# First output tile finished and stored in column halves, and 8 KB store runs for two batches only

## The chip, the cores and the metric

The kernel runs on one core of a Trainium2 chip. The metric is the device time of one execution in microseconds (us); the lower, the better. Times quoted as "span" are of one profiled execution, from its first to its last instruction, and are 1.7 to 1.9 us shorter than the device time.

## The reference, cut to what matters

```python
# linear attention with elu+1 features -> x, shape (8, 576, 512); then:
X = np.fft.rfft(x, axis=1)                 # along the sequence
Y = np.zeros_like(X)
Y[:, :64] = X[:, :64] times w_r + i*w_i    # one complex 512x512 matrix per mode
u = x + np.fft.irfft(Y, n=576, axis=1)
out = u + np.maximum(u @ w_ch, 0.0)        # float32
```

## The kernel before

For 380 us the kernel streams the mode matrices (64 modes, two 1 MB matrices each) from HBM, the chip's main memory. Everything that doesn't need the last modes is done meanwhile: each output tile (128 rows x 512 columns) already holds x plus the inverse transform of most modes, and `E0` holds most of its channel product. The last 8 modes arrive at the end. Their rows are in `last`: `last[:, 0]` is the spectrum, `last[:, 1]` the same times `w_ch`. Then, for each pair of tiles, TensorE forms an accumulator in two banks of PSUM, the memory that TensorE writes its sums to (`channels`: E0 through an identity, then the inverse transform of the second part of `last` or of `YZ_all`, the copy of `last` spread out by batch). ScalarE rectifies it in place, TensorE adds the inverse transform of the first part, VectorE adds x, and SyncE stores the pair.

```python
    QUADS = (2, 4, 5, 6)        # batches whose 4 main tiles go in one store of 8 KB runs

    def finish(n: int):
        add_inverse(n, 0)
        ...
        on_bank(n, {0, 1}, nc.vector.tensor_tensor(out=x, in0=acc, in1=x, op=ALU.add))
        if t0 < B * NJJ and t0 // NJJ in QUADS:
            if t0 % NJJ:
                store(t0 - 2, NJJ)       # 1 MB, only when the second pair is done
            return
        store(t0, 2)                     # 0.5 MB, 4 KB runs

    # ---- the last modes have come; rows[] are their transposed spectrum
    for h in range(2):
        for ec in range(NDC):
            pin(nc.tensor.matmul(last_ps[h][:, 0:hw], rows[ec], wch16[:, ec, COLS[h]], ...))   # zl, then z1l
        pin(nc.scalar.copy(out=last[:, 1, COLS[h]], in_=last_ps[h][:, 0:hw]))
    pin(nc.tensor.matmul(y0, lead_sb[0][:, rows_of(0)], last[:, 0, :]))
    pin(nc.vector.tensor_tensor(out=x_of(0), in0=y0, in1=x_of(0), op=ALU.add))
    for h, eng in enumerate((nc.sync, nc.gpsimd)):
        eng.dma_start(out=YZ_all[...], in_=last...)
    psW.release()                        # y0's pool; its banks become accumulators 2 and 3
    ...
    add_inverse(0, 1)
    on_bank(0, {0}, nc.vector.scalar_tensor_tensor(      # x += max(acc, 0)
        out=x_of(0), in0=accs[0][:, 0], scalar=0.0, in1=x_of(0), op0=ALU.max, op1=ALU.add))
    store(0, 1)
    relu(0, 1)
    rectified(1)
    channels(2)
    ...
```

Also of interest later: `FILL` gives the number of filler matmuls after each pair of modes, which keep TensorE busy while it waits for weights.

```python
    FILL = {**{p: 5 for p in range(18, 27)}, 27: 8, 28: 2, 29: 7, 30: 7}
```

## Time and profile before

| | |
|---|---|
| device time, median of 4 runs | 425.81 us (424.87 to 425.96) |
| span of the profiled run | 422.9 us |
| last cast that the change doesn't reach (VectorE, 128x64 into Y) starts | 390.18 us |
| first store issued | 393.51 us |
| TensorE's last matmul ends | 414.3 us |
| last data packet ends | 421.5 us |

The cast into Y is the last step common to all kernels, so I measure from it: the **tail** is the stretch from its start to the end of the span, 32.74 us here.

These two rows of the page of before show 40 equal slices of the span, in tenths: the clock granted to TensorE, and the busy share of the 16 DMA engines.

```profile
...
PEclk9999778869855555555555598999799896899997
DMA  9999999999999999999999999999999999996797
...
```

DMA is busy nearly always: the kernel is bound by its transfers, and only the few slices at the end can be changed by this edit. The windows view of before cuts them finer. Each row gives a stretch in us, its length, each engine's busy time with its number of instructions, the granted clock, the DMA share and GB/s. (A packet counts whole in the stretch in which it starts, so a share can come out just over 1.)

```profile
...
core 0: us, PE busy (x) PEld busy (x) DVE busy (x) ACT busy (x) POOL busy (x), PEclk, DMA share, GB/s
398.00:400.00 2.00, 2.00 (x13) 0.53 (x10) 2.00 (x3) 1.72 (x5) 0.00 (x0) 1.00 0.96 384
400.00:401.00 1.00, 1.00 (x10) 0.34 (x9) 1.00 (x1) 0.76 (x2) 0.00 (x0) 1.00 0.90 365
401.00:402.00 1.00, 1.00 (x9) 0.28 (x8) 0.97 (x2) 0.86 (x3) 0.00 (x0) 1.00 0.26 107
402.00:403.00 1.00, 1.00 (x9) 0.27 (x6) 0.95 (x2) 0.98 (x2) 0.00 (x0) 1.00 0.99 418
403.00:420.00 17.00, 10.82 (x60) 2.67 (x56) 12.47 (x11) 9.64 (x18) 0.00 (x0) 0.90 1.00 400
420.00:421.00 1.00, 0.00 (x0) 0.00 (x0) 0.00 (x0) 0.00 (x0) 0.00 (x0) 0.50 0.07 29
421.00:422.00 1.00, 0.00 (x0) 0.00 (x0) 0.00 (x0) 0.00 (x0) 0.00 (x0) 0.50 0.03 12
...
```

There is a dry stretch: DMA share 0.26 in 401 to 402 us, because the 1 MB store of batch 2 waits for its second pair. From 402 to 420 us the transfers never stop. From 420 us a single engine is left (0.07 of 16 is about one).

The timeline of before at the start of the tail (start, length, engine, line, operation, tiles, shapes, count, and in brackets the idle time before with what ended it):

```profile
...
start us, us, engine line op out<-in xcount [idle before <-releaser]
...
391.77 0.37 ACT L918 CAST last<-z1l 128x256 f16<-128x256 f32 x1
391.99 0.69 DVE L920 TENSOR_TENSOR x_main<-y0l,x_main 128x512 f32<-128x512 f32 x1 [0.80 <-PE y0l L919]
392.17 0.64 SPq L922 DMA_DIRECT2D YZ_all<-last  x1
...
392.79 0.69 DVE L943 SCALAR_TENSOR_TENSOR x_main<-acc,x_main 128x512 f32<-128x512 f32 x1
...
393.05 0.59 PE L775 MATMUL acc<-E,id 128*128 128x512 f16 x2
...
393.51 0.34 SPq L791 DMA_DIRECT2D out_dram<-x_main  x1
393.92 0.69 DVE L937 TENSOR_TENSOR x_main<-acc,x_main 128x512 f32<-128x512 f32 x1 [0.44 <-PE acc L736]
```

ScalarE casts z1l at 391.77 us, which completes `last`; accumulator 2 starts on TensorE at 393.05 us (L775); VectorE makes two full passes over the first tile; SyncE copies `last` into YZ_all and then stores the first tile.

### The profile page before, as it was taken

How to read it: one execution, taken by the hardware profiler on the slowest of the kernel's cores; microseconds unless marked ns; L12 is line 12 of the kernel's file. 1: busy time of each engine (PE TensorE's matmuls, PEld its weight loads, DVE VectorE, ACT ScalarE, POOL GpSimd, SP SyncE). 2: the span in 40 equal slices, each digit the busy share in tenths (PEclk: the TensorE clock that was granted, in tenths of full speed). 3: DMA queues.
4: the chain of work that ended last, by engine and by line, in shares of the span. 5: the costliest groups of instructions: out<-in, count | busy, mean ns of one | idle time of the engine just before them, and what ended most of it. 6: DMA issues, size and time to landing. Idle time of an engine off the chain costs nothing.

```text
span 422.9 us, 7976 instructions
## 1 busy us (share of the span) xinstructions
PE 279.6 (66%) x3426; PEld 153.2 (36%) x3426; DVE 215.4 (51%) x446; ACT 161.7 (38%) x253; POOL 56.5 (13%) x99
## 2 busy tenths in 40 slices
PE   1358387788717645344344768878798886989991
PEld 0246366666402322222122333334243333465320
DVE  4599488886202453354444434454264333423892
ACT  4688578754201102000000234444254351331881
POOL 4222124210000111111011111110110001130000
PEclk9999778869855555555555598999799896899997
DMA  9999999999999999999999999999999999996797
GB/s 217 210 208 215 207 220 202 224 209 222 221 215 219 207 215 217 222 211 217 218 212 217 217 220 214 215 216 215 214 219 220 215 212 219 223 201 126 248 409 287
DMA packets 20227, 93.20 MB, mean 220 GB/s; under 512 B 2016, under 2 KB 11104, under 8 KB 15520
## 3 DMA queue, kind: packets, MB, share of 16 engines
q0 software_dynamic: 16512, 81.47, 94.0%
q1 hardware_dynamic: 3680, 11.22, 7.0%
q8 instruction: 27, 0.44, 0.4%
q14 instruction: 8, 0.07, 0.0%
HBM read 163.93 MB, written 9.44 MB: 410 GB/s over the span
## 4 chain that ended last, share of the span: by engine, by line
DMA 63%; PE 22%; DVE 4%; ACT 3%; issue 2%; POOL 2%; DVEq 0%; POOLq 0%; ACTq 0%
DMA w<-in_moe_w_i_dram 48%; DMA pick_sb<-row_pick 8%; PE P L442 7%; DMA k<-in_k_dram 7%; PE acc L736 3%; PE acc L775 2%; PE zl L425 2%; ACT ke L213 2%; POOL w L119 1%; PE eps L677 1%; DVE ys L452 1%; PE ya L654 1%; PE yt L460 1%; PE xTp L667 1%; PE z L699 1%
## 5 line engine op out<-in xcount | busy, mean ns | idle before, releaser
L442 PE MATMUL P<-w,xt_c 64*32 64x512 bf16 (+2 forms) x1000 | 50.2, 531 | 59.7 <-DMA w<-in_moe_w_i_dram 58.3
L452 DVE CAST ys<-P 128x512 f16<-128x512 f32 x32 | 22.1, 692 | 122.2 <-PE P L442 122.2
L454 ACT CAST ys<-P 128x512 f16<-128x512 f32 x31 | 18.1, 585 | 154.1 <-PE P L442 154.1
L119 POOL DMA_DIRECT2D w<-in_moe_w_r_dram x31 | 16.6, 534 | 246.2 <-PE P L442 96.4
L442 PEld LDWEIGHTS <-xt_c 64*32 64x32 bf16 (+2 forms) x1000 | 16.7, 127 | 79.8 <-DMA w<-in_moe_w_i_dram 44.6
L165 PEld LDWEIGHTS <-qT 64*128 64x128 f16 (+1 forms) x640 | 23.0, 123 | 49.8 <-issue 31.0
L677 PE MATMUL eps<-wch,xTw 128*128 128x512 f16 x144 | 40.2, 406 | 0.0
L165 PE MATMUL num<-kv,qT 64*128 64x65 f16 (+1 forms) x320 | 13.7, 209 | 25.4 <-ACT xt_c L350 12.0
L658 DVE TENSOR_TENSOR x_main<-ya,x_main 128x512 f32<-128x512 f32 x32 | 22.0, 689 | 13.4 <-PE ya L654 13.2
L660 ACT CAST x16w<-x_main 128x512 f16<-128x512 f32 x32 | 19.8, 618 | 23.4 <-DVE x_main L658 22.3
L165 PE MATMUL nw<-kv,qT 64*128 64x65 f16 (+1 forms) x320 | 19.0, 240 | 9.5 <-DVE x_tail L621 4.3
L685 ACT CAST E<-eps 128x512 f16<-128x512 f32 (+1 forms) x40 | 21.2, 540 | 8.5 <-PE eps L677 8.4
L299 DVE TENSOR_TENSOR x<-num,rd 128x512 f16<-128x512 f32 x32 | 22.1, 692 | 1.1
L242 PE MATMUL qTp<-id,qe 128*128 128x128 f16 x144 | 16.1, 301 | 9.9 <-DVE qe L226 9.4
L460 PE MATMUL yt<-pick_sb,ys 128*128 128x16 f16 x252 | 11.7, 174 | 16.3 <-DMA pick_sb<-row_pick 9.6
L213 ACT ACTIVATE qe<-q 128x1152 f16<-128x1152 f16 (+1 forms) x16 | 17.9, 1157 | 10.4 <-DMA q<-in_q_dram 6.5
L249 ACT COPY qT<-qTp 128x1152 f16<-128x1152 f16 x16 | 19.6, 1287 | 0.7 <-PE qTp L242 0.2
L425 PE MATMUL zl<-wch,id 128*128 128x512 f16 x72 | 19.6, 408 | 0.0
L213 ACT ACTIVATE ke<-k 128x1152 f16<-128x1152 f16 x16 | 17.7, 1152 | 4.9 <-DMA k<-in_k_dram 4.9
L460 PEld LDWEIGHTS <-ys 128*128 128x128 f16 x252 | 9.7, 102 | 26.4 <-DVE ys L452 15.0
L785 ACT ACTIVATE acc<-acc 128x512 f32<-128x512 f32 x34 | 18.1, 582 | 2.4 <-PE acc L736 1.6
L242 PEld LDWEIGHTS <-qe 128*128 128x128 f16 x144 | 13.8, 140 | 11.0 <-DVE qe L226 9.8
(113 smaller groups left out, 468.6 us busy)
## 6 DMA issues: line engine op xcount, KB each, us to landing
w<-in_moe_w_r_dram POOLq DMA_DIRECT2D x31, 1024.0 KB, 12.5
w<-in_moe_w_i_dram POOLq DMA_DIRECT2D x31, 1024.0 KB, 17.0
k<-in_k_dram POOLq DMA_DIRECT2D x8, 576.0 KB, 12.8
v<-in_v_dram POOLq DMA_DIRECT2D x8, 576.0 KB, 14.8
out_dram<-x_main SPq DMA_DIRECT2D x4, 1024.0 KB, 4.9
q<-in_q_dram POOLq DMA_DIRECT2D x7, 576.0 KB, 12.9
out_dram<-x_main SPq DMA_DIRECT2D x6, 512.0 KB, 4.6
q<-in_q_dram SPq DMA_DIRECT2D x2, 576.0 KB, 4.3
```

The lines of the kernel that those rows point to most:

```text
L119: nc.gpsimd.dma_start(out=w_in[p][half::2], in_=two.rearrange("g (r dc) e -> (g r) dc e", dc=NDW))
L165: mm = nc.tensor.matmul(num[hpo][orow, c0 : c0 + 65], qT[rows, hpp, h2, cols], kv_sb[rows, hpp, h2, :])
L213: pin(nc.scalar.activation(out=ev[:, c], in_=heads(nm, b, c), func=AF.Exp))
L242: nc.tensor.transpose(qT_ps[:, j], phi["q", b][:, c, j].rearrange("p o d -> p (o d)"), id16,)
L299: nc.vector.tensor_tensor(out=dst.rearrange("p (o c d) -> p o c d", o=2, c=4), in0=nv[:, :, :, 0:64], in1=rden.unsqueeze(3).broadcast_to([ ...
L425: pin(nc.tensor.matmul(last_ps[0], id16, wch16[:, 0, :]))
L442: nc.tensor.matmul(P[c : c + n, :], xt_cols(dc, kk, n), w[rows, dc, :], start=(dc < NDC), stop=(dc >= n_dc - NDC), tile_position=(rows.sta ...
L452: pin(nc.vector.tensor_copy(out=st, in_=P))
L460: nc.tensor.matmul(yt_ps[:, ec, kk % 8, :], st[:, ec * 128 : ec * 128 + 128], pick_sb)
L658: pin(nc.vector.tensor_tensor(out=x, in0=acc, in1=x, op=ALU.add))
L677: nc.tensor.matmul(e_ps, xT[:, c, :], wch16[:, c, :], start=(c == 0), stop=(c == NDC - 1))
L685: pin(nc.scalar.copy(out=dst, in_=e_ps[:, cols]))
```

## The change

The intent is to get the first store out sooner and to smooth the stores. The first tile is finished in two column halves. VectorE can then work on the first half while TensorE still completes the second, and to allow that the second half's sum gets a PSUM bank of its own. The Trainium skill ("PSUM — Partial Sum Buffer", Terms) says that TensorE writing and VectorE reading one bank and quadrant at once is a collision error. Batches 2 and 4 are stored pair by pair (4 KB runs), only 5 and 6 in 8 KB runs.

```diff
--- before.py
+++ after.py
@@ -799,7 +799,7 @@
             in_=x_tail[i // 2],
         )
 
-    QUADS = (2, 4, 5, 6)
+    QUADS = (5, 6)
 
     def finish(n: int):
         acc = accs[n]
@@ -907,6 +907,17 @@
         pin(nc.tensor.transpose(y_ps[ec // 2][:, ec % 2, :], rows[ec], id16))
     pin(nc.scalar.copy(out=last[:, 0, COLS[0]], in_=y_ps[0].rearrange("p c r -> p (c r)")))
     pin(nc.vector.tensor_copy(out=last[:, 0, COLS[1]], in_=y_ps[1].rearrange("p c r -> p (c r)")))
+    z0 = psW.tile([128, D], F32, tag="P", bufs=2, name="z0h1")[:, COLS[1]]
+
+    def second_half_sums():
+        pin(nc.tensor.matmul(z0, id16, e0_parts(0)[0][1][:, COLS[1]], start=True, stop=False))
+        pin(
+            nc.tensor.matmul(
+                z0, inv2_sb[0 : 2 * NF, rows_of(0)], YZ[0][0 : 2 * NF, 1, COLS[1]],
+                start=False, stop=False,
+            )
+        )
+
     for h in range(2):
         for ec in range(NDC):
             pin(
@@ -916,8 +927,29 @@
                 )
             )
         pin(nc.scalar.copy(out=last[:, 1, COLS[h]], in_=last_ps[h][:, 0:hw]))
-    pin(nc.tensor.matmul(y0, lead_sb[0][:, rows_of(0)], last[:, 0, :]))
-    pin(nc.vector.tensor_tensor(out=x_of(0), in0=y0, in1=x_of(0), op=ALU.add))
+        if h == 0:
+            pin(nc.tensor.matmul(y0, lead_sb[0][:, rows_of(0)], last[:, 0, :]))
+            second_half_sums()
+    for h in range(2):
+        x = x_of(0)[:, COLS[h]]
+        l, r = lead_sb[0][:, rows_of(0)], last[:, 1, COLS[h]]
+        if h == 0:
+            z = accs[0][:, 0, COLS[0]]
+            on_bank(0, {0}, nc.tensor.matmul(z, l, r, start=False, stop=True, skip_group_check=True))
+        else:
+            z = z0
+            pin(nc.tensor.matmul(z, l, r, start=False, stop=True))
+        pin(nc.vector.tensor_tensor(out=x, in0=y0[:, COLS[h]], in1=x, op=ALU.add))
+        ins = nc.vector.scalar_tensor_tensor(
+            out=x, in0=z, scalar=0.0, in1=x, op0=ALU.max, op1=ALU.add
+        )
+        if h == 0:
+            on_bank(0, {0}, ins)
+        else:
+            pin(ins)
+        nc.sync.dma_start(
+            out=out_rows[0:512, COLS[h]].rearrange("(r j) d -> r j d", j=NJJ)[:, 0, :], in_=x
+        )
     for h, eng in enumerate((nc.sync, nc.gpsimd)):
         eng.dma_start(
             out=YZ_all[64 * h : 64 * h + 64 : NF // NL].rearrange("r b z d -> r b (z d)"),
@@ -937,14 +969,7 @@
         on_bank(n, {i}, nc.vector.tensor_tensor(out=x_of(t), in0=accs[n][:, i], in1=x_of(t), op=ALU.add))
         store(t, 1)
 
-    add_inverse(0, 1)
-    on_bank(
-        0, {0},
-        nc.vector.scalar_tensor_tensor(
-            out=x_of(0), in0=accs[0][:, 0], scalar=0.0, in1=x_of(0), op0=ALU.max, op1=ALU.add
-        ),
-    )
-    store(0, 1)
+    add_inverse(0, 1, (1,))
     relu(0, 1)
     rectified(1)
     channels(2)
```

## The prediction

> **What bounds the kernel now.** On the page the DMA row reads 9 in nearly every slice, and in the chain of waits the weight load ends at 380.5 us; the change touches only what follows. From 380.5 to 411.9 us the chain is TensorE, then two VectorE adds and the last stores (span 422.9 us). The windows view splits this tail:
> - 390 to 392 us: no DMA. First store issued at 393.51 us (timeline, SyncE).
> - 398 to 402 us: DMA follows compute. Pairs leave VectorE every 1.22 us (0.5 MB each); the 1 MB store of batch 2 waits for its second pair, to 401.07 us. DMA share in 401 to 402 us is 0.26: with its edges, about 1.1 us lost.
> - 403 to 420 us: DMA share 1.00, 400 GB/s, never dry again: the bytes left at 402 us set the end. The Trainium skill ("DMA: Bandwidth & Descriptors", Specifications) gives a fabric ceiling of 435 GB/s; the trace stays under it.
> - One DMA engine fetches 16 KB of instructions at 414 us and ends about 1.2 us after the others. I expect that to stay.
>
> **What the change does.**
> 1. Batch 2 leaves in two 0.5 MB stores, the first at about 399.9 us before any new delay: the dry stretch is filled. Gain 0.9 to 1.1 us, on the critical path.
> 2. Batches 2 and 4 go in 4 KB rather than 8 KB runs. Packets take about 160 and 309 ns: 2 MB cost about 0.2 us more.
> 3. On TensorE, y0 and two new matmuls (0.11 us each, estimated as half a 512-column one) now stand before the second group of z1l. ACT casts that at about 392.30 instead of 391.77 us, and whatever needs all of `last` waits: z0, the remaining inverse sums, both YZ_all copies (issued at 392.7 instead of 392.17 us). VectorE makes four half passes of about 0.43 us (estimate from 225 ns for 64 columns and 692 ns for 512) instead of two of 0.69, so the next accumulator gets its banks only at about 393.7 us. TensorE was busy without a break, so later pairs come 0.4 to 0.7 us later.
> 4. SyncE still issues the YZ_all copy first (0.64 us), so the halves leave at about 393.3 and 393.7 us: nearly nothing gained over 393.51.
>
> **Sum.** The queue becomes continuous from the first pair of batch 1, which arrives later than now: 1.1 saved, minus about 0.55, minus about 0.2. Net gain about 0.3 us (0.1%); three runs of before spread by 1.0 us.
>
> Predicted 425.4 us, 80% range 424.6 to 426.2. Chances: faster by over 2% 0.01, within 2% 0.98, slower 0.01.
>
> **What would show it.** Windows: DMA share in 401 to 402 us rises to about 1; in 398 to 399 us it falls. Timeline: batch 2's first store at about 400.5 us, ACT's second z1l cast at 392.3 us, batch 1's first store at about 398 instead of 397.44 us. If batch 1's stores aren't later, step 3 is wrong and the gain is nearer 0.8 us. If the DMA share stays low near 401 us, step 1 is wrong.
>
> **What would make it wrong.** YZ_all lands at about 396.3 us for a use at 396.51; with half-tile stores beside it TensorE could stall and eat the gain. The instruction fetch may fall on another moment and move the end by up to 1 us. The 380 us before may vary by more.

## The result, and the profile after

| | before | after |
|---|---|---|
| device time, median of 4 | 425.81 us | 425.91 us (425.42 to 426.86) |
| ratio | | 1.001 (95%: 0.9986 to 1.0033) |
| span of the profiled run | 422.9 us | 425.0 us |
| cast into Y starts | 390.18 us | 391.56 us |
| tail | 32.74 us | 33.41 us |

A ratio is the mean time of one kernel's fast runs over that of the other's in the same rounds, so it isn't quite the ratio of the medians. The time is the same within 2%. The median lies inside the forecast range, but the forecast gain of 0.3 us isn't there: if anything, the kernel is slower. The two profiles differ by 2.1 us, of which only 0.67 us lie in the tail. The other 1.4 us lie before the cast, in code that the change doesn't touch. The windows of before, then of after, show why:

```profile
...
378.00:380.00 2.00, 1.43 (x7) 0.46 (x5) 0.00 (x0) 0.44 (x1) 0.00 (x0) 1.00 0.96 201
...
381.00:384.00 3.00, 3.00 (x56) 2.14 (x40) 1.02 (x2) 1.17 (x2) 0.00 (x0) 1.00 1.00 207
...
```

```profile
...
378.00:380.00 2.00, 0.52 (x3) 0.03 (x1) 0.00 (x0) 0.00 (x0) 0.00 (x0) 1.00 0.94 197
...
381.00:384.00 3.00, 3.00 (x46) 1.49 (x32) 1.09 (x2) 0.58 (x1) 0.00 (x0) 0.50 1.00 206
...
```

In after's profile TensorE had been idle for longer (busy 0.52 of 2 us, against 1.43) and then ran at clock 0.50 from 381 to 384 us. The unchanged kernel did the same in its second profile (below), so the change isn't needed for it.

The windows of after, shifted by the 1.38 us by which its cast is later:

```profile
...
399.38:401.38 2.00, 2.00 (x12) 0.54 (x12) 1.90 (x3) 1.74 (x4) 0.00 (x0) 1.00 0.97 380
401.38:402.38 1.00, 1.00 (x8) 0.31 (x4) 1.00 (x2) 0.98 (x3) 0.00 (x0) 1.00 0.99 401
402.38:403.38 1.00, 1.00 (x10) 0.34 (x8) 0.97 (x2) 0.75 (x2) 0.00 (x0) 1.00 1.01 406
403.38:404.38 1.00, 1.00 (x9) 0.24 (x7) 1.00 (x1) 0.86 (x3) 0.00 (x0) 1.00 1.00 406
404.38:421.38 17.00, 11.65 (x66) 2.92 (x62) 13.25 (x12) 10.46 (x20) 0.00 (x0) 0.91 1.00 397
421.38:422.38 1.00, 0.00 (x0) 0.00 (x0) 0.00 (x0) 0.00 (x0) 0.00 (x0) 0.50 0.20 76
422.38:423.38 1.00, 0.00 (x0) 0.00 (x0) 0.00 (x0) 0.00 (x0) 0.00 (x0) 0.50 0.05 20
...
```

The dry stretch is gone, as predicted. (The fall of the share at 398 to 399 us, which the prediction listed as another sign, didn't come: counted from the cast, that stretch has 0.94 in both.) But the drain in the next 17 us runs on past its old end: share 0.20 and 0.05 in the last two rows, against 0.07 and 0.03. The timeline of after at the start of the tail shows the price:

```profile
...
392.87 0.27 PE L913 MATMUL z0h<-E,id 128*128 128x256 f16 x1
393.07 0.11 PEld L915 LDWEIGHTS <-inv_sb 64*128 64x128 f16 x1 [0.32 <-issue]
393.07 0.42 DVE L942 TENSOR_TENSOR x_main<-y0l,x_main 128x256 f32<-128x256 f32 x1 [0.50 <-PE y0l L931]
393.08 0.30 PE L915 MATMUL z0h<-YZ_all,inv_sb 64*128 64x256 f16 x1
...
393.95 0.37 ACT L929 CAST last<-z1l 128x256 f16<-128x256 f32 x1 [0.86 <-PE z1l L924]
394.06 0.42 DVE L943 SCALAR_TENSOR_TENSOR x_main<-acc,x_main 128x256 f32<-128x256 f32 x1 [0.57 <-PE acc L938]
394.35 0.62 SPq L954 DMA_DIRECT2D YZ_all<-last  x1
...
394.40 0.41 DVE L942 TENSOR_TENSOR x_main<-y0l,x_main 128x256 f32<-128x256 f32 x1
...
394.92 0.42 DVE L943 SCALAR_TENSOR_TENSOR x_main<-z0h,x_main 128x256 f32<-128x256 f32 x1
...
395.03 1.70 SPq L950 DMA_DIRECT2D out_dram<-x_main  x2
395.40 0.59 PE L775 MATMUL acc<-E,id 128*128 128x512 f16 x2
...
396.25 0.69 DVE L969 TENSOR_TENSOR x_main<-acc,x_main 128x512 f32<-128x512 f32 x1 [0.90 <-PE acc L736]
```

Counted from the cast, the z1l cast of ScalarE comes at 2.39 us (1.59 in before), accumulator 2 at 3.84 us (2.87), and the first store of batch 1, which opens the unbroken stretch of transfers, at 8.10 us (7.27). The critical chain of after (start, length, what) shows what accumulator 2 waits for, VectorE's last half pass:

```profile
...
394.92 0.44 DVE x_main L943
395.36 0.04 issue
395.40 0.59 PE acc L775 x2
...
```

The first half tile is stored at 3.47 us, later than the whole tile in before (3.33 us), because SyncE still issues the YZ_all copy first and that needs all of `last`.

One more difference is at the very end. SyncE's waits from 416 us on, before and then after (who waits for what: us in total, times, longest):

```profile
...
SPq L991 <- DMA out_dram<-x_main: 4.3, 3, 1.9
SPq L991 <- DMA out_dram<-x_tail: 1.2, 1, 1.2
...
```

```profile
...
SPq L1016 <- DMA out_dram<-x_main: 5.3, 1, 5.3
...
```

SyncE ends the program by waiting for its eight DMA semaphores (counters that a transfer raises when it lands) in a fixed order. Stores take the semaphores in turn. In before the last store has the sixth, so SyncE works through the order while the transfers land (three waits for main stores and one for a tail store). In after, with 19 stores instead of 16, the last store has the first semaphore: one wait of 5.3 us, and the other seven are done afterwards, about 0.06 us each in the trace's records. From the last packet to the end of the span it is 1.43 us in before and 1.71 us in after.

### The profile page after: what moved, and what is told of

It reads as the page before. It is cut to its first block, busy times and chain, and to the rows that moved or that the text cites. A ratio compares the mean times of both kernels' runs of the same rounds, so it can differ in the third digit from the quotient of the medians.

```text
span 425.0 us, 7990 instructions
## 1 busy us (share of the span) xinstructions
PE 278.9 (66%) x3429; PEld 152.0 (36%) x3429; DVE 215.6 (51%) x448; ACT 161.5 (38%) x253; POOL 56.3 (13%) x99
## 4 chain that ended last, share of the span: by engine, by line
DMA 63%; PE 21%; DVE 5%; ACT 4%; issue 2%; POOL 2%; DVEq 0%; POOLq 0%; ACTq 0%
DMA w<-in_moe_w_i_dram 48%; DMA pick_sb<-row_pick 8%; PE P L442 8%; DMA k<-in_k_dram 7%; PE acc L736 3%; PE acc L775 2%; PE zl L425 2%; ACT ke L213 2%; POOL w L119 1%; PE eps L677 1%; ACT qT L249 1%; DVE ys L452 1%; PE z L699 1%; PE yt L460 1%; DVE x L299 1%
```

## The experiments

All in one table; every time is counted from the start of the cast into Y and worked out from the trace's records. "14 done" is when 14 of the 16 DMA engines have written their last completion. The gap from there to "last packet" is the lag of the slowest engine. A half clock *inside* the tail spoils the early columns; it is marked.

| run | cast at | z1l cast | acc. 2 starts | first batch-1 store | 14 done | last packet | then to end | tail |
|---|---|---|---|---|---|---|---|---|
| before | 390.18 | 1.59 | 2.87 | 7.27 | 30.05 | 31.31 | 1.43 | 32.74 |
| c1_before_again | 391.55 | 1.59 | 2.88 | 7.27 | 30.09 | 31.46 | 1.41 | 32.87 |
| after | 391.56 | 2.39 | 3.84 | 8.10 | 30.21 | 31.70 | 1.71 | 33.41 |
| c1_after_again | 391.29 | 2.39 | 3.84 | 8.09 | 30.17 | 31.75 | 1.72 | 33.47 |
| c1_halves_only | 391.55 | 2.39 | 3.84 | 8.09 | 30.86 | 32.19 | 1.33 | 33.52 |
| c1_runs_only (half clock) | 390.11 | 2.64 | 4.18 | 8.57 | 30.62 | 32.09 | 1.32 | 33.41 |
| c3_runs_only2 | 391.10 | 1.59 | 2.87 | 7.27 | 29.30 | 30.94 | 1.30 | 32.24 |
| c2_no_sums | 390.45 | 1.94 | 3.39 | 7.65 | 29.71 | 31.33 | 1.72 | 33.05 |
| c2_sums_first | 391.69 | 2.34 | 3.51 | 7.90 | 29.93 | 31.42 | 1.76 | 33.18 |
| c3_late_sums | 391.45 | 1.59 | 3.62 | 7.89 | 29.94 | 31.43 | 1.75 | 33.18 |
| d1_late_adds | 391.51 | 1.59 | 3.08 | 7.35 | 29.40 | 30.87 | 1.75 | 32.62 |
| c2_after_q456 | 390.38 | 2.39 | 3.84 | 8.09 | 30.25 | 31.87 | 1.30 | 33.17 |
| c2_no_fetch (half clock) | 390.19 | 2.63 | 3.92 | 8.31 | 30.87 | 31.05 | 1.35 | 32.40 |
| c3_after_no_fetch (half clock) | 390.14 | 3.72 | 5.59 | 10.27 | 32.33 | 33.68 | 1.73 | 35.41 |
| d1_after_trim (half clock) | 390.01 | 3.23 | 4.82 | 9.11 | 31.15 | 31.30 | 1.66 | 32.97 |
| c3_runs_no_fetch | 390.08 | 1.59 | 2.87 | 7.27 | 29.27 | 29.31 | 1.27 | 30.58 |
| d1_best_warm | 390.28 | 1.59 | 2.87 | 7.26 | 29.46 | 30.98 | 1.34 | 32.31 |
| e1_best30 (half clock) | 390.06 | 1.64 | 3.72 | 8.51 | 30.53 | 30.56 | 1.26 | 31.81 |
| e1_best30_warm | 391.72 | 1.59 | 2.87 | 7.26 | 29.29 | 29.54 | 1.25 | 30.79 |

My theory (A): the stores of batch 2 gain what I said, and the halves lose it again by delaying the accumulators behind the first tile. Rivals: the 4 KB runs cost the gain (B), the change brings the half clock (C), the end of the program costs it (D, which turned out a part of the truth), the fetch of a block of instructions costs it. The expectations call "theory E" the view that this fetch holds one DMA engine back in both kernels and isn't the change's loss.

### The two parts alone, with both kernels as controls

`c1_before_again` and `c1_after_again` are the two kernels unchanged. `c1_runs_only` is before with one line:

```diff
-    QUADS = (2, 4, 5, 6)
+    QUADS = (5, 6)
```

`c1_halves_only` is after with that line the other way round.

> Control: the kernel before, unchanged. Tail means the stretch from the start of the last VectorE cast of the mode products (the 128x64 cast into Y) to the end of the span; it was 32.7 us in the profile of before and 33.4 us in that of after. Both theories expect a ratio of 1.000 within 0.002 and a tail of 32.7 us within 0.2. Anything larger is what this measurement can't resolve.

> Control: the changed kernel, unchanged. Theory A (the change gains about 0.9 us by filling the dry DMA stretch and loses 1.0 us or more by delaying the first tiles; the half clock at 381 to 384 us in its first profile, 1.4 us, was chance): tail 33.4 us within 0.2, first batch-1 store about 0.8 us later after the last cast than in before, ratio 1.000 to 1.002. Rival C (the change itself brings the half clock): the half clock near 381 us is there again and the ratio is 1.003 or more.

> Kernel before with the store-run line alone (batches 2 and 4 in 4 KB runs). Theory A: dry stretch filled, nothing else moved: tail about 31.8 us, 0.9 us less than before; ratio about 0.998; first batch-1 store unmoved relative to the last cast; DMA share near 1 in the 2 us after the store of the second pair of batch 1. Rival B (4 KB runs cost in the drain what the filled stretch gains): tail about 32.7 us, ratio 1.000.

> Changed kernel with the old store-run line (batches 2 and 4 in 8 KB runs again). Theory A: the delay of about 0.8 us stays and the dry stretch is back: tail about 33.9 us (33.5 to 34.2), ratio about 1.002 to 1.003. Rival B (halves cost nothing, runs cost it all): tail 32.7 us, ratio 1.000.

Ratios: before again 1.0012 (0.9997 to 1.0026), after again 1.0025 (1.001 to 1.0039), runs alone 0.9994 (0.9977 to 1.0011), halves alone 1.0025 (1.0008 to 1.0041). The first is the same kernel as its comparison, so 0.1% is what such a comparison can't resolve. The tails can: in the two pairs of profiles at hand they repeat within 0.13 us. After is 0.60 to 0.67 us longer than before, pair by pair; the halves alone 0.65 to 0.78 us (a tail of 33.52 us, at the low edge of the 33.5 to 34.2 expected). Rival C fell as a full account: the half clock came in the control c1_before_again (at 382.5 us) and not near there in c1_after_again. In all the profiles with every filler in place it came at 380.8 to 382.5 us in 2 of 4 with the first tile whole and in 5 of 8 with it halved; whether the change makes it likelier, so few can't tell.

The profile of `c1_runs_only` fell on a half clock at 390.3 us, inside the tail, so it was run again as `c3_runs_only2`.

> Kernel before with the store-run line alone, again, as its first profile fell on a half clock at 390.3 us and hides the tail. Theory A at full clock: first batch-1 store at 7.27 us, most engines done at 29.4 to 29.6 us (30.05 in before), tail 32.0 to 32.3 us, ratio 0.998 to 0.999. Rival B: tail 32.7 us. If the half clock is there again: first batch-1 store at 8.6 us and tail 33.4 us.

Ratio 0.9988 (0.9974 to 1.0003), tail 32.24 us: 0.5 to 0.6 us shorter than before, with the head unmoved. The windows of this run, counted on from its cast as above:

```profile
...
398.92:400.92 2.00, 2.00 (x13) 0.52 (x10) 2.00 (x3) 1.72 (x5) 0.00 (x0) 1.00 0.96 385
400.92:401.92 1.00, 1.00 (x11) 0.34 (x9) 1.00 (x1) 0.76 (x2) 0.00 (x0) 1.00 0.99 397
401.92:402.92 1.00, 1.00 (x10) 0.28 (x8) 0.97 (x2) 0.86 (x3) 0.00 (x0) 1.00 1.02 414
402.92:403.92 1.00, 1.00 (x9) 0.26 (x6) 0.95 (x2) 0.99 (x2) 0.00 (x0) 1.00 1.01 401
...
```

The share stays near 1 where it was 0.26. Against before, 14 engines are done 0.75 to 0.79 us sooner, but the slowest engine then lags by 1.64 us instead of 1.26 to 1.37. Rival B fell as stated (the tail isn't 32.7 us), though a third to a half of the gain is lost to the lag. The end wait gave 0.11 to 0.13 us of it back: with 18 stores it is 1.30 us, by the order of waits described above and not by the drain. So the store-run line gains about 0.5 us and the halves lose more than that.

### Where the halves lose it

`c2_no_sums` leaves out the two new matmuls (its second half is wrong). `c2_sums_first` only moves them ahead of y0. Accumulators 2 and 3 take over the banks of y0 and of the second half (z0), and this move swaps which takes which.

```diff
# c2_no_sums
-            second_half_sums()
-            pin(nc.tensor.matmul(z, l, r, start=False, stop=True))
+            pin(nc.tensor.matmul(z, l, r, start=True, stop=True))
# c2_sums_first
-            pin(nc.tensor.matmul(y0, lead_sb[0][:, rows_of(0)], last[:, 0, :]))
             second_half_sums()
+            pin(nc.tensor.matmul(y0, lead_sb[0][:, rows_of(0)], last[:, 0, :]))
```

> Changed kernel without the two new matmuls (second half of the first tile takes the last product alone; wrong on purpose in 128 rows x 256 columns). All times from the start of the cast into Y. Theory A1 (the two matmuls cost 0.43 us of TensorE time ahead of z1l, twice my estimate): first batch-1 store at 7.7 us (8.10 in after, 7.27 in before), second z1l cast at 1.95 us (2.39 in after, 1.59 in before), tail 33.0 us. Rival A2 (the bank's late release by VectorE is the whole delay): first batch-1 store stays at 8.0 to 8.1 us.

> Changed kernel with the two new matmuls ahead of y0; the third and fourth tile of the rotation then change places, so the next accumulator no longer waits for the bank of the second half but only for TensorE, and VectorE's release is waited for one accumulator later. Theory A2 (bank release): accumulator 2 starts without a wait at about 3.5 us after the cast (3.84 in after, 2.87 in before), first batch-1 store at about 7.8 us. Rival A1 (matmuls alone): first batch-1 store stays at 8.0 to 8.1 us.

Without the matmuls the first batch-1 store comes at 7.65 us (0.45 sooner), with the swap at 7.90 us (0.20 sooner). Both A1 and A2 hold in part, neither alone. Ratios 1.0008 (0.9993 to 1.0024) and 1.0006 (0.9987 to 1.0024) can't tell them apart.

`c3_late_sums` moves y0 and the sums behind both z1l groups, so that ScalarE's cast is as early as in before. `d1_late_adds` also puts VectorE's two y0 adds ahead of its two rectified adds.

```diff
# c3_late_sums
-        if h == 0:
-            pin(nc.tensor.matmul(y0, lead_sb[0][:, rows_of(0)], last[:, 0, :]))
+        if h == 1:
             second_half_sums()
+            pin(nc.tensor.matmul(y0, lead_sb[0][:, rows_of(0)], last[:, 0, :]))
# d1_late_adds, besides
+    for h in range(2):
+        x = x_of(0)[:, COLS[h]]
+        pin(nc.vector.tensor_tensor(out=x, in0=y0[:, COLS[h]], in1=x, op=ALU.add))
     for h in range(2):
         ...
-        pin(nc.vector.tensor_tensor(out=x, in0=y0[:, COLS[h]], in1=x, op=ALU.add))
```

> Changed kernel with y0 and the two new matmuls after both z1l groups, the sums ahead of y0. Times from the start of the cast into Y. Theory A (the order on TensorE and the bank wait make the delay, not the halves themselves): second z1l cast at 1.6 us as in before, accumulator 2 at 2.9 to 3.0 us, first batch-1 store at 7.3 to 7.5 us (8.10 in after), most DMA engines done at about 29.5 us, tail 32.3 to 32.5 us with the long end wait of 1.7 us still in it. Rival F (four half passes on VectorE are the delay): first batch-1 store at 7.8 us or later.

> Changed kernel with y0 and the sums after both z1l groups (as in the late-sums run) and both y0 adds of VectorE ahead of its two rectified adds, so that y0's bank, which the next accumulator takes over, is read out after two half passes instead of three. Times from the cast into Y. Theory F' (the next accumulator waits for VectorE's serial half passes over the bank it takes over): accumulator 2 starts at 3.15 to 3.25 us (3.62 with the late sums alone, 2.87 in before), first batch-1 store at 7.4 to 7.6 us (7.89). Rival F (total VectorE work decides): first batch-1 store stays at 7.8 to 7.9 us.

The cast was back at 1.59 us in both. But with the late sums accumulator 2 still started at 3.62 us, not at the 2.9 to 3.0 I had expected: a miss. The TensorE timeline of c3_late_sums names the wait, and that of d1_late_adds shows it gone:

```profile
...
395.07 0.61 PE L775 MATMUL acc<-E,id 128*128 128x512 f16 x2 [0.52 <-DVE x_main L942]
...
```

```profile
...
394.59 0.60 PE L775 MATMUL acc<-E,id 128*128 128x512 f16 x2
...
```

TensorE stood for 0.52 us until VectorE's second y0 add was through. It is the third of four half passes in the order of the change, and accumulator 2 inherits y0's bank. With the two adds first, the accumulator started at 3.08 us (expected 3.15 to 3.25) and the first batch-1 store came at 7.35 us (7.27 in before). The total VectorE work is the same in both runs, so rival F fell. The tail was 32.62 us, 0.8 us shorter than after's; the ratio, 1.0008 (0.999 to 1.0027), doesn't resolve that. (The ratio of c3_late_sums, 1.0007, 0.999 to 1.0024, tells no more.) Even so 14 engines were done at 29.40 us, no sooner than with the store-run line alone (29.30 us): halving the first tile gained nothing even with its delay mended.

### The end of the program

`c2_after_q456` is after with `QUADS = (4, 5, 6)`: one store fewer, which moves the last store from the first semaphore to the eighth.

> Changed kernel with batch 4 back in one 8 KB-run store: one SyncE transfer fewer, so the last store has the last of the eight semaphores that SyncE waits for at the end, not the first. Theory D (each wait after the last landing costs 0.06 us): last packet to end of span 1.3 us (1.71 in after, 1.43 in before), tail 33.0 us. Rival: last packet to end stays at 1.7 us because it depends on the store itself.

From the last packet to the end it took 1.30 us, as theory D has it. The tail was 33.17 us, not 33.0: the last packet came 0.17 us later than in after; the ratio, 1.0006 (0.9991 to 1.002), can't show it. In the table this interval goes with the kernel's number of stores: 1.66 to 1.76 us in all eight profiles with 19 stores, 1.25 to 1.43 us in all eleven with 16, 17 or 18.

### The instruction fetch

A 16 KB packet of instructions occupies one DMA engine for 0.88 us in the drain of before. The DMA view of before from 413.9 to 415 us (queue, packets, MB, share of 16 engines):

```profile
...
q1 hardware_dynamic: 51, 0.41, 93.0%
q8 instruction: 1, 0.02, 5.0%
...
```

`c2_no_fetch` is before with 10 filler matmuls (20 TensorE instructions) fewer; `c3_after_no_fetch` is the same for after; `c3_runs_no_fetch` the same with the store-run line alone.

```diff
-    FILL = {**{p: 5 for p in range(18, 27)}, 27: 8, 28: 2, 29: 7, 30: 7}
+    FILL = {**{p: 5 for p in range(20, 27)}, 27: 8, 28: 2, 29: 7, 30: 7}
```

> Kernel before with 10 filler matmuls (20 TensorE instructions) fewer at pairs 18 and 19. Theory E (the 16 KB instruction fetch at 414 us is TensorE's, triggered within the last dozen of its instructions, and holds one DMA engine 1.2 us behind): no such fetch, all engines end together about 30.1 us after the cast, tail 31.5 us, ratio 0.997. Rival: the fetch only comes earlier or belongs to another engine, tail stays at 32.7 us. If the fillers hold the clock up, earlier parts get slower: seen in the time of the cast (390.1 to 391.5 us in the runs so far).

> Changed kernel without the 16 KB fetch (10 filler matmuls fewer). Theory E: all engines end together near 30.2 us after the cast, tail 31.9 us, ratio about 0.998 to 0.999, so that the change's loss against the likewise trimmed before stays at about 0.5 us (delay and end wait) and the fetch explains the rest of the 0.67. Rival: the loss vanishes with the fetch, then the tail is 31.4 us as in a trimmed before.

> Candidate to beat both: store-run line alone plus 10 filler matmuls fewer. At full clock most engines and the last packet end near 29.5 us, tail 30.9 to 31.1 us, ratio 0.995 to 0.996. With the half clock in the tail 32.2 us. If only one of the two gains counts, the ratio is 0.997 as in the run without the fetch alone.

In c2_no_fetch the fetch was gone, the lag fell to 0.18 us, and the ratio was 0.9969 (0.9954 to 0.9984), though its profile had a half clock in the tail and so a tail of 32.40 us instead of the 31.5 expected. In c3_after_no_fetch the fetch was still there, at 416.3 us: after has 6 TensorE instructions more, so the cut was too small, and a 6.8 us half clock spoiled the tail besides (ratio 1.0018, 1.0002 to 1.0035). c3_runs_no_fetch was the best so far: ratio 0.9952 (0.9937 to 0.9967), tail 30.58 us. The DMA view of its last 8 us holds no instruction packet (one follows at 421.6 us, after the program's end), and its windows show all engines ending together:

```profile
...
q1 hardware_dynamic: 752, 2.88, 84.0%
...
```

```profile
...
418.00:419.00 1.00, 0.00 (x0) 0.00 (x0) 0.00 (x0) 0.00 (x0) 0.00 (x0) 0.50 1.00 403
419.00:420.00 1.00, 0.00 (x0) 0.00 (x0) 0.00 (x0) 0.00 (x0) 0.00 (x0) 0.50 0.24 90
420.00:421.00 1.00, 0.00 (x0) 0.00 (x0) 0.00 (x0) 0.00 (x0) 0.00 (x0) 0.50 0.00 0
...
```

`d1_after_trim` took 15 fillers (30 instructions) from after, at pairs 18 to 20.

> Changed kernel with 15 filler matmuls fewer (30 TensorE instructions; 20 were not enough for it, as it has 6 more than before). Theory E: the 16 KB fetch no longer falls before the last store; all engines end near 30.2 us after the cast, tail 31.9 to 32.0 us at full clock, ratio 0.998 to 0.999, so about 0.6 us slower than the likewise trimmed before (0.9969). Rival: the loss was the fetch, ratio 0.997.

The fetch had moved to 424.7 us, behind the end of the program's own instructions (423.0 us), and the lag was 0.15 us. The ratio was 0.9992 (0.9972 to 1.0011), the tail unusable for the half clock. The trimmed before, measured against before on another chip, had 0.9969. So the loss hardly was the fetch, but the intervals overlap, and time alone doesn't settle it. Two things blur it further. In three of the six runs of d1_after_trim the device time is 2.4 to 2.9 us longer than the span, not 1.7 to 1.9, so there something outside the span took time; whether it is the late fetch, no run shows. And fewer fillers may cost clock: of the five profiles with fillers only taken away, four have a half clock at 389.7 to 391.4 us, in or just before the tail; of the twelve with all fillers, one has.

`d1_best_warm`, `e1_best30` and `e1_best30_warm` look for the best version: all have `QUADS = (5, 6)`.

```diff
+    FILL = {20: 1, **{p: 5 for p in range(21, 27)}, 27: 8, 28: 2, 29: 7, 30: 11}   # d1_best_warm
+    FILL = {**{p: 5 for p in range(21, 27)}, 27: 8, 28: 2, 29: 7, 30: 7}           # e1_best30
+    FILL = {21: 1, **{p: 5 for p in range(22, 27)}, 27: 8, 28: 2, 29: 7, 30: 11}   # e1_best30_warm
```

> Candidate: store-run line alone, 14 filler matmuls fewer at pairs 18 to 20 and 4 more at pair 30, where TensorE waits 1.0 to 2.2 us for the last weights. Theory G (a wait of about 1.5 us or more there brings a half clock for 3.4 us and costs 1.3 us): no half clock between 375 and 390 us, runs no longer spread over 1.2 us (422.7 to 424.0 us without the filler), ratio 0.994. Rival: the spread stays, ratio 0.995.

> Store-run line alone with 15 filler matmuls (30 TensorE instructions) fewer. Theory E (where the 16 KB fetch falls is a matter of how many TensorE instructions are left; 20 fewer was the edge, as one profile had it at 31.5 us and one at 27.1 us after the cast): no fetch before the last store's landing, all engines end together, tail 30.6 us at full clock or 31.9 us with the half clock in the tail, ratio 0.995. Rival (the fetch falls at random): a fetch at 24 to 28 us after the cast and a tail of 32.2 us.

> The same 15 fewer in sum, with 4 filler matmuls more at pair 30 and 19 fewer at pairs 18 to 21. Theory G (a wait of about 1.5 us or more before the last weights brings the half clock): no half clock from 375 us to the end of TensorE's work, tail 30.6 us, runs spread by less than 1 us, ratio 0.994. Rival: spread over 1 us, ratio 0.995, and fewer fillers at pairs 18 to 21 cost nothing either way.

With 20 instructions fewer the fetch of d1_best_warm came at 417.4 us, still before the last store had landed: tail 32.31 us, ratio 0.9959 (0.994 to 0.9978). With 30 fewer neither profile had it before the end: lags of 0.03 and 0.25 us, ratios 0.9954 (0.9936 to 0.9972) and 0.995 (0.9932 to 0.9967). No half clock lay between 375 us and the end of TensorE's work in either warm profile, as theory G has it, but the runs still spread by 1.6 us (423.51 us median, 422.67 to 424.28), so the extra fillers didn't show a gain. Theory G isn't shown either: c3_runs_no_fetch waited 1.57 us there without them and had no half clock. The best version beats before by about 0.5%, 2.1 us, and c3_runs_no_fetch, without extra fillers, does the same within the intervals.

## Why the prediction was right or wrong

Two parts of the prediction failed. The term "minus about 0.55" (step 3, later pairs) measured 0.83 us, which leaves nearly nothing of the gain. And the sum took all that follows the bytes left at 402 us as unchanged ("One DMA engine [...] ends about 1.2 us after the others. I expect that to stay"): the lag grew by 0.21 to 0.23 us and the wait at the program's end by 0.28 to 0.31 us, which turned a gain of about nothing into a loss. Term by term:

- **The dry stretch (step 1): right.** The DMA share in it went from 0.26 to about 1.0.
- **Smaller runs (step 2): undersized.** Store-run line alone: I had 0.9 us in sum for steps 1 and 2. 14 engines gained 0.75 to 0.79 us, the whole tail 0.5 to 0.6 us. In all full-clock profiles with the fetch inside the drain, the slowest engine lags by 1.26 to 1.37 us where four batches go in 8 KB runs and by 1.47 to 1.64 us where two or three do (the half-clock profile of c3_after_no_fetch, with two, has 1.35). Why a fetch costs more beside 4 KB runs, no run shows.
- **The delay of later pairs (step 3): right in kind, mis-sized.** The prediction put "about 0.55" into the sum; it measured 0.83 us (first batch-1 store 7.27 to 8.10). Two terms were short. The two matmuls delay z1l by 0.44 us, twice my 0.22 (their starts at 392.87 and 393.08 us, z1l's at 393.31): the weights of the 64-row matmul load only at 393.07 us, 0.20 us after the matmul before it began, with PEld idle for 0.32 us until then. And accumulator 2 waits for VectorE's last half pass, which ends at 3.78 us after the cast, not 3.5. Taking these away one by one moved the store by 0.45 and 0.20 us; the order of d1_late_adds took away 0.75 of the 0.83 us.
- **The first half's store (step 4): nearly right.** I said that the halves leave at about 3.1 and 3.5 us after the cast and that nearly nothing is gained on the whole tile's 3.33; they left at 3.47 and 4.08.
- **Missing from the sum: the end.** The order of the eight last waits cost 0.28 to 0.31 us. I had not looked there.
- **The sum.** Tail of after against before, profile by profile in their two pairs: 14 engines done +0.16 and +0.08 us, lag +0.23 and +0.21 us, end wait +0.28 and +0.31 us; together +0.67 and +0.60 us, where I had -0.3. The model of the drain itself was sound: with the measured 0.75 to 0.79 us for steps 1 and 2 and 0.83 us for step 3 it gives a loss of 0.04 to 0.08 us for the first of these terms.
- **The warnings.** YZ_all landing late didn't matter; TensorE had no wait for it. The part before the cast did vary by 1.4 us, more than all this, as I had said.

Shown by runs: the gain of the store line, the delay and its two causes, the end wait, each by a tail or two at full clock and not by device times, which can't resolve them. That the median lay in the forecast range says little: the range was 1.6 us wide, and the four runs of one kernel spread by 1.1 to 1.4 us. Only read from the pattern of profiles: the larger lag beside 4 KB runs. Still open: its mechanism, and what brings the half clock.

## What to carry to other kernels

Work put ahead of a critical step on a full engine cost twice here (0.45 and 0.20 us): by its own time, and by the time at which its last reader releases the bank that the next stage takes over; so order the readers by who waits for the bank. When stores drain at the end, fill the dry stretches, then look at the one DMA engine that ends last and at what the program does after the last landing. When single runs differ by more than the effect, measure from the last common instruction.

## What the Trainium skill lacked or had wrong

- "Runtime: NRT & Kernel Launch", Instruction fetch mechanics: it says that crossing a 16 KiB boundary is mostly hidden. The 16 KB blocks agree with the trace (16,384 bytes, 0.88 to 1.42 us on one DMA engine in the tail's neighbourhood), but in every profile with such a fetch inside the saturated drain the last engine ended 1.26 to 1.64 us behind 14 of the others, and in those without one 0.03 to 0.25 us. Ending the program of before 20 TensorE instructions sooner, which took the fetch out, gave a ratio of 0.9969.
- "TensorE: Matmul & The Clock Gate", Part 1 and the table of "Why this matters for your kernels": half clock after an idle window of about 3.4 us, and advice to avoid gaps over about 3 us. The lengths of the half clock agree with a window of 3.4 us (3.41, 6.83 and 10.24 us in the traces). But no gap of that length was needed here: at 380.8 to 382.5 us it came after single TensorE gaps of 1.47 to 2.21 us in seven profiles, gaps of 1.41 and 1.57 us had none, and in five profiles it came at 389.7 to 391.4 us with no gap over 0.73 us in the 12 us before. So the length of one gap doesn't tell when it comes; that the gaps cause it was not tested. (The same page tells of another kernel whose many short idles had this effect, but gives no length for them.)
- "DMA: Bandwidth & Descriptors", Specifications: the row for HBM gives about 358 GB/s per core. The drain of before wrote 400 GB/s over 17 us. That is no contradiction, as the page says under its measured bandwidths that this is the share when both cores of a domain stream, and this kernel runs on one core; the row alone doesn't say so. The fabric ceiling of 435 GB/s held.
- No page I found tells that SyncE's waits for its DMA semaphores at the program's end run in a fixed order, so that the number of stores shifts the end by 0.3 us (1.43 us with the last store on the sixth semaphore, 1.71 with it on the first).
